# Attention: the narrow transposes of a slot share one PSUM buffer, and the exponentials come first in every slot

## The chip, the cores and the metric

The kernel runs on one core of a Trainium2 chip. The metric is the device time of one execution in microseconds (us). Before the change it is 1161.03 us, the median of three runs (1156.31, 1161.03 and 1164.13).

## The reference, cut to what matters

Attention with a learned bias from relative positions, then two feed-forward blocks on its output (B = 4, H = 8, S = 576, D = 64; 2304 tokens, 512 columns). The change is in the first block alone.

```python
scores = scale * np.matmul(q, k.transpose(0, 1, 3, 2)) + bias
scores = scores - np.max(scores, axis=-1, keepdims=True)
attn = np.exp(scores)
attn = attn / (np.sum(attn, axis=-1, keepdims=True) + 1e-09)
x = np.matmul(attn, v)                       # block 1: attention
h = x @ w_in                                 # block 2
x = (h * np.clip(h + 3.0, 0.0, 6.0) / 6.0) @ w_out
out = (sigmoid(x @ w_gate) * (x @ w_val)) @ w_out2   # block 3
```

## The kernel before, in words

The program has a bias stage (to about 57 us), the attention (57 to about 340 us), the first feed-forward block and the gated one. Attention works on 16 units; a unit n is a pair of heads of one batch. A unit has nine steps s: steps 0 to 7 are a block of 128 query rows of one head (chunk c = s // 2, head h = s % 2), and step 8 holds the last 64 rows of both heads. The 144 steps t run in slots of two: `slot_of_two(i)` (L508) does in slot i, in this order of the text:

- `scores` (L374) of steps 2i and 2i+1: 4 matmuls each (10 for step 8) into a tile `s` of two PSUM banks (two such tiles), then on VectorE (DVE) one custom instruction (L388) that adds the bias into `u` and finds the row's bound. A score tile is free again when its `u` is made.
- In every slot that is in the table `AV` (L498): the 20 matmuls of P times V for half of the query columns of a unit (`av`, L466), and on DVE the product with the inverse sums (`av_out`, L490). Slots with and without this work alternate, but two slots without it follow each other once in nine: modulo 9 the slots 5, 7, 1 and 3 have it. Here they are called AV slots.
- `expo` (L402): the exponential of the slot's two steps on ScalarE (ACT, L404), with the row sums.
- `invert` (L407), one slot after step 5 or 8 of a unit: reciprocal sums on DVE, spread over `spread` by ACT copies (L415).
- `turn_inv` (L417), two slots after step 5 or 8: TensorE (PE) transposes 3 or 2 blocks of `spread` into a PSUM tile `tr`, which ACT and DVE evict to `inv`.
- `trans` (L438) of the two steps of the slot before: 4 transposes of the probabilities `p` (or `pm`, for step 8) into a tile `tr`, evicted to `ptm` by DVE or ACT (the table `PT_EVAC`: steps 1, 3, 5, 7 by ACT, 0, 2, 4, 6 by DVE; step 8 by ACT in odd units).
- `trans_rem` (L454): the narrow rest, one transpose per chunk (and one of `pm` with the fourth chunk), evicted to `ptr`. The rest of chunk 0 of the next unit shares the tile of the second `turn_inv` (`beside`).
- `prep` and `load_qk`: splitting Q and K of the next unit (casts on ACT at L336, products on GpSimd, POOL) and loading those of the one after.

`tr` is a ring of three banks (`bufs=3`): a transpose into a new tile waits until the tile taken three times earlier is evicted. PE's order is that of the text (`in_turn` ties each matmul to the one before). On the other engines a scheduler sets the order at build time. Between these, ten weights of the next block are prepared (`load.one_step`, L689: a DMA `raw`, an `Abs` on ACT at L174, DVE work at L178 to L190, a cast on ACT at L206).

The exponentials have two places: at their place above when the slot is an AV slot or the next is none (L522), and else at the end of the slot, tied behind the last ACT eviction (L543):

```python
        for t in steps(i) if i not in AV and i + 1 in AV else ():
            with ExitStack() as order:
                if last_e:
                    order.enter_context(tc.issue_after(last_e[-1].ins))
                expo(t)
```

Of the kernel before, what the change touches and what calls it, by code (L numbers as in the profile page):

```python
# [10 lines left out]
F32 = mybir.dt.float32  # L11
# [7 lines left out]
P = 128  # L19
B, H, S, D = 4, 8, 576, 64  # L20
# [21 lines left out]

PREP_ON = "APPP"
PT_EVAC = "VAVAVAVAA"


NPRE = 10
# [49 lines left out]
def block_kernel(ctx: ExitStack, tc: tile.TileContext, q, k, v, mlp, w_in, w_out, w_gate, w_val, w_out2, dist_d,  # L97
                 rows_d, out):
    nc = tc.nc
# [253 lines left out]
    ptm = apool.tile([P, 2, 4, S], F32, name="ptm")  # L353
    ptr = apool.tile([P, S], F32, name="ptr")
    pts, us, avs, last_u, last_pe = {}, {}, {}, [None], []
    last_e = []

    @contextmanager
    def in_turn():
# [54 lines left out]
            i = sums[n % 3][:, s0:s1].unsqueeze(2).to_broadcast(o.shape)  # L414
            nc.scalar.copy(o, i)  # L415

    def turn_inv(n, c0, c1):  # L417

        ps = pp.tile([P, 4, P], F32, name="tr", bufs=3)
        for c in range(c0, c1):  # L420
            with in_turn() as done:
                done(nc.tensor.transpose(ps[:, c % 3], spread[:, P * c : P * c + P], ident))
        if c1 == 3:
            evac("A", inv[:, 0 : 3 * P].rearrange("p (c q) -> p c q", c=3), ps[:, 0:3])
        else:
            evac("V", inv[:, 3 * P : 4 * P], ps[:, 0])
            for h in range(2):
                r = slice(64 * h, 64 * h + 64)
                evac("VA"[h], inv[r, 4 * P : S], ps[r, 1, r])
            return ps  # L430

    def evac(eng, dst, src):
        if eng == "A":
            last_e.append(nc.scalar.copy(dst, src))  # L434
        else:
            nc.vector.tensor_copy(dst, src)  # L436

    def trans(t):  # L438
        n, s = seq[t]
        if s < 8:  # L440
            ps = pp.tile([P, 4, P], F32, name="tr", bufs=3)
            c, h = divmod(s, 2)
            for kc in range(4):
                with in_turn() as done:
                    done(nc.tensor.transpose(ps[:, kc], pts[n, c][:, h, 64 * h + P * kc : 64 * h + P * kc + P], ident))  # L445
            evac(PT_EVAC[s], ptm[:, h, :, P * c : P * c + P], ps)
        else:
            ps = pp.tile([P, 4, P], F32, name="tr", bufs=3)
            for kc in range(4):
                with in_turn() as done:  # L450
                    done(nc.tensor.transpose(ps[:, kc], Pm[n % 2][:, P * kc : P * kc + P], ident))
            evac("VA"[n % 2], ptm[:, :, :, 512:S], ps.rearrange("p c (h q) -> p h c q", h=2))

    def trans_rem(n, c, beside=None):  # L454

        ps = pp.tile([P, 4, P], F32, name="tr", bufs=3) if beside is None else beside[:, 2:4]
        with in_turn() as done:
            done(nc.tensor.transpose(ps[:, 0], pts[n, c].rearrange("p h s -> p (h s)")[:, 512 : 512 + P], ident))
        if c == 3:
            with in_turn() as done:  # L460
                done(nc.tensor.transpose(ps[0:64, 1], Pm[n % 2][:, 512:S], ident))
            for h in range(2):
                evac("AV"[h], ptr[64 * h : 64 * h + 64, 512:S], ps[0:64, 1, 64 * h : 64 * h + 64])
        evac("A", ptr[:, P * c : P * c + P], ps[:, 0])

    def av(n, a, g):  # L466
        if g == 0:
# [37 lines left out]
    def steps(i):  # L505
        return [t for t in (2 * i, 2 * i + 1) if 0 <= t < NS]

    def slot_of_two(i):  # L508

        for t in steps(i):  # L510
            scores(t)
            n, s = seq[t]
            p, b = divmod(n, B)
            if s == 0:
                last_v[0] = load_v(n)
            if b == B - 1 and p + 1 < NPAIR and (s % 2 == 1 or s == 8):
                load_bias(p + 1, s // 2)
        for n, a, g in AV.get(i, ()):
            av(n, a, g)
            if g == 4:  # L520
                av_out(n, a)
        for t in steps(i) if i in AV or i + 1 not in AV else ():  # L522
            expo(t)
        for t in steps(i - 1):
            n, s = seq[t]
            if s in (5, 8):
                invert(n, s // 6 * 3, s // 6 * 2 + 3)
        beside = None
        for t in steps(i - 2):
            n, s = seq[t]  # L530
            if s in (5, 8):
                beside = turn_inv(n, s // 6 * 3, s // 6 * 2 + 3)
        for t in steps(i - 1):
            n, s = seq[t]
            trans(t)
            if s in REM and (s < 8 or n % 2 == 0):
                trans_rem(n, REM[s], beside)
                beside = None
        for t in steps(i - 2):
            n, s = seq[t]  # L540
            if s == 8 and n % 2:
                trans_rem(n, REM[s])
        for t in steps(i) if i not in AV and i + 1 in AV else ():  # L543
            with ExitStack() as order:
                if last_e:
                    order.enter_context(tc.issue_after(last_e[-1].ins))
                expo(t)
        for t in steps(i):
            if t in PREP:
                n, h = PREP[t]  # L550
                prep(n, h)
            for k, (n, h) in PREP.items():
                if h == 1 and n + 1 < NU and t == k + 3:
                    load_qk(n + 1)
# [426 lines left out]
```

## Time and profile before

| | us |
|---|---|
| median of three runs | 1161.03 |
| the profiled execution, its own time | 1163.19 |
| its span (first to last instruction) | 1161.4 |
| PE busy in the span | 1121.8 (97%) |
| attention (57 to 340 us): length, PE busy | 283.0, 263.1 |
| attention: ACT busy, DVE busy | 221.5, 211.1 |
| the rest after attention (340 to 1161 us): length, PE busy | 821.0, 813.2 |

The page gives busy time by engine. A view by windows gives the same for a stretch; the list of waits says which engine stood idle until which other engine's instruction ended; the timeline gives the instructions of one engine in order of time, neighbours of a kind merged into one row with a count. "L458" is line 458 of the kernel. A name such as `tr` stands for all buffers of that name. PE's granted clock is 0.99 to 1.00 throughout.

### The profile page before, as it was taken

What the parts mean: (1) busy time and instruction counts of PE and PEld (TensorE: products, weight loads), DVE (VectorE), ACT (ScalarE), POOL (GpSimd) and SP (SyncE); (2) the same over time, 40 slices, a digit from 0 to 9 for tenths busy, and PEclk for the clock granted to TensorE, in tenths of its full rate; (3) what the DMA queues carried; (4) which work ended last, traced back from release to release, by engine and by line L of the source; (5) the groups of instructions that cost most, each with busy time, mean ns of one, the idle gap of its engine ahead of it and who ended that gap; (6) DMA issues with size and microseconds to landing.
All of it is one profiled execution on the core that took longest, in us unless ns stands there. A gap on an engine that the chain in (4) does not pass through costs nothing.

```text
span 1161.4 us, 19270 instructions
## 1 busy us (share of the span) xinstructions
PE 1121.8 (97%) x6878; PEld 1013.5 (87%) x6878; DVE 762.8 (66%) x1487; ACT 585.8 (50%) x1288; POOL 422.8 (36%) x340
## 2 busy tenths in 40 slices
PE   8799999989999999999999999999999999999998
PEld 3287777767779999999999999989899898998997
DVE  8977777787768887356377685575357656643443
ACT  7988877877855455454455445333333222221221
POOL 0154635635206443231346445261333313311211
PEclk9999999999999999999999999999999999999999
DMA  6855436364113565349566659976868748757532
GB/s 203 298 160 143 143 102 194 95 184 128 33 38 109 201 213 194 118 154 327 185 240 233 255 184 347 397 259 256 334 251 303 298 167 312 281 187 258 190 109 73
DMA packets 83503, 236.82 MB, mean 204 GB/s; under 512 B 9936, under 2 KB 12624, under 8 KB 83408
## 3 DMA queue, kind: packets, MB, share of 16 engines
q1 hardware_dynamic: 83408, 235.60, 58.3%
q8 instruction: 54, 0.88, 0.3%
q14 instruction: 41, 0.34, 0.1%
HBM read 154.15 MB, written 81.41 MB: 203 GB/s over the span
## 4 chain that ended last, share of the span: by engine, by line
PE 79%; DVE 6%; ACT 6%; DMA 4%; issue 2%; POOL 1%; SPq 0%; ACTq 0%; POOLq 0%; DVEq 0%
PE o L728 17%; PE h L862 11%; PE o L862 10%; PE o L917 6%; PE h L917 6%; PE h L664 5%; PE h L665 5%; PE h L663 5%; PE s L384 4%; PE av L475 4%; DMA raw<-in_part_dram 3%; PE tr L445 2%; ACT p L404 2%; DVE u L388 2%; DVE ptm L436 1%
## 5 line engine op out<-in xcount | busy, mean ns | idle before, releaser
L728 PE MATMUL o<-gh,slot 128*128 128x384 f32 x768 | 195.9, 335 | 1.8 <-DVE take L436 1.8
L728 PEld LDWEIGHTS o<-gh,slot 128*128 128x128 f32 x768 | 139.2, 188 | 2.2 <-DVE take L436 2.1
L728 PE MATMUL o<-gl,slot 128*128 128x384 f32 x384 | 129.1, 336 | 0.7 <-DVE gl L714 0.7
L388 DVE CUSTOM_DVE_ANT_0 u<-s,bias 128x576 f32<-128x576 f32 x128 | 94.2, 754 | 26.1 <-ACT p L404 12.1
L384 PE MATMUL s<-k,q 128*128 128x288 f32 (+2 forms) x672 | 106.3, 303 | 0.8 <-ACT ptm L610 0.4
L898 POOL TENSOR_TENSOR gp<-s,gp 128x384 fp32r<-128x384 f32 x36 | 39.4, 1107 | 176.8 <-ACT gp L897 91.7
L404 ACT ACTIVATE p<-u,stat 128x576 f32<-128x576 f32 x128 | 98.1, 773 | 11.0 <-DVE stat L388 10.7
L670 DVE SCALAR_TENSOR_TENSOR g<-g,h 128x384 f32<-128x384 f32 x94 | 51.5, 548 | 70.4 <-ACT g L669 70.3
L714 DVE TENSOR_TENSOR gl<-g,gh 128x384 fp32r<-128x384 f32 x94 | 63.2, 672 | 47.9 <-ACT gh L713 46.1
L713 ACT CAST gh<-g 128x384 fp32r<-128x384 f32 x94 | 48.2, 513 | 91.3 <-DVE g L670 91.0
L384 PEld LDWEIGHTS s<-k,q 128*128 128x128 f32 x672 | 91.5, 190 | 1.6 <-DVE stat L388 0.8
L207 POOL TENSOR_TENSOR hl<-corners,hl 128x512 fp32r<-128x512 f32 x42 | 57.3, 1368 | 94.2 <-ACT hl L206 79.2
L669 ACT ACTIVATE g<-h,half 128x384 f32<-128x384 f32 x94 | 54.5, 580 | 58.8 <-PE h L665 58.3
L862 PE MATMUL o<-x,slot 128*128 128x384 f32 x432 | 78.0, 335 | 0.0
L862 PE MATMUL h<-x,slot 128*128 128x384 f32 x432 | 77.8, 335 | 0.0
L862 PEld LDWEIGHTS h<-x,slot 128*128 128x128 f32 x432 | 75.2, 188 | 0.7
L207 POOL TENSOR_TENSOR slot<-z,slot 128x512 fp32r<-128x512 f32 x19 | 28.5, 1503 | 129.7 <-ACT slot L206 129.7
L862 PEld LDWEIGHTS o<-x,slot 128*128 128x128 f32 x432 | 75.1, 188 | 0.0
L445 PE MATMUL tr<-ident,p 128*128 128x128 f32 x512 | 73.3, 277 | 1.4 <-ACT ptr L434 1.3
L728 PEld LDWEIGHTS o<-gl,slot 128*128 128x128 f32 x384 | 72.4, 189 | 1.3 <-DVE gl L714 1.3
L898 POOL TENSOR_TENSOR x<-s,x 128x384 fp32r<-128x384 f32 x36 | 40.2, 1130 | 81.7 <-ACT x L897 48.3
L475 PE MATMUL av<-ptm,vn 128*64 128x288 f32 x512 | 69.2, 413 | 0.0
(154 smaller groups left out, 2708.7 us busy)
## 6 DMA issues: line engine op xcount, KB each, us to landing
w<-hl SPq DMA_DIRECT2D x67, 512.0 KB, 3.4
slot<-w SPq DMA_DIRECT2D x67, 512.0 KB, 5.8
raw<-in_part_dram SPq DMA_DIRECT2D x50, 512.0 KB, 4.2
x<-xc SPq DMA_DIRECT2D x56, 384.0 KB, 5.9
sum<-sum SPq DMA_DIRECT2D x72, 256.0 KB, 3.4
early<-xc SPq DMA_DIRECT2D x28, 384.0 KB, 6.0
nbias<-ptm SPq DMA_DIRECT2D x36, 295.5 KB, 3.1
early<-in_part_dram SPq DMA_DIRECT2D x32, 288.0 KB, 4.4
```

Of the source, the lines that this page charges most:

```text
L207: eng.tensor_tensor(out=slot[:, 1], in0=z, in1=slot[:, 0].bitcast(F32), op=ALU.subtract)
L384: done(nc.tensor.matmul(ps[:, a, o : o + w], Q[:, q0 : q0 + P], K[:, r, h, k0 : k0 + w], start=(i == 0), stop=(i == len(mm) - 1)))
L388: last_u[0] = nc.vector.tensor_tensor_reduce(out=halves(u), in0=ps[:, :, 0:HS], in1=halves(bt), op0=ALU.add, op1=ALU.min, scale=-0.125, sc ...
L404: nc.scalar.activation(probs(t), us.pop(t), AF.Exp, bias=low[n % 2][:, s : s + 1], scale=-1.0, accum_out=sums[n % 3][:, s : s + 1])
L445: done(nc.tensor.transpose(ps[:, kc], pts[n, c][:, h, 64 * h + P * kc : 64 * h + P * kc + P], ident))
L475: done(nc.tensor.matmul(ps[64 * h : 64 * h + 64, 0:HS], vt[:, 4 * h + g], ptm[:, h, g, cols], start=(g == 0), stop=False))
L663: nc.tensor.matmul(ps[:, 0:TW], wh, XH[:, c], start=(c == 0), stop=False)
L714: last_g[0] = nc.vector.tensor_tensor(out=gl, in0=g, in1=gh.bitcast(F32), op=ALU.subtract)
L728: nc.tensor.matmul(os[c][:, 0:TW], sl[:, r, P * c : P * c + P], x, start=(first and r == 0 and x is gh), stop=(last and x is gl))
L862: nc.tensor.matmul(ps[b], sl[:, r, o : o + P], x[:, c, s], start=(k < 4 and i == 0), stop=(i == len(mm) - 1), skip_group_check=True)
L898: nc.gpsimd.tensor_tensor(out=G[:, i, 1], in0=s, in1=G[:, i, 0].bitcast(F32), op=ALU.subtract)
L917: nc.tensor.matmul(os[i], x[:, P * i : P * i + P], slots[(base + 14 + e) % NALL][:, r], start=first, stop=last)
```

## The change

There are three parts. (1) `turn_inv` and `trans_rem` no longer take a tile and evict at once. They are given a tile and a column, do their transposes, and return a function that evicts. `turn_narrow` collects the narrow transposes of a slot in one tile `tr` of four columns, makes all of them, and then does all evictions. (2) Their place moves: the inverse sums now come after the wide transposes of the slot, and for odd units those of step 8 come three slots later rather than two. (3) All exponentials are at their first place, and the tie to the last ACT eviction is gone. No arithmetic is added or left out. Over two units 27 tiles `tr` are taken rather than 28.

```diff
+    def turn_inv(n, c0, c1, ps, at):
         for c in range(c0, c1):
+            turn(ps[:, at + c - c0], spread[:, P * c : P * c + P])
+        def out():
+            if c1 == 3:
+                evac("A", inv[:, 0 : 3 * P].rearrange("p (c q) -> p c q", c=3), ps[:, at : at + 3])
+            else:
+                evac("V", inv[:, 3 * P : 4 * P], ps[:, at])
...
+        return out
...
-    def trans_rem(n, c, beside=None):
-        ps = pp.tile([P, 4, P], F32, name="tr", bufs=3) if beside is None else beside[:, 2:4]
+    def trans_rem(n, c, ps, at):
+        turn(ps[:, at], pts[n, c].rearrange("p h s -> p (h s)")[:, 512 : 512 + P])
         if c == 3:
+            turn(ps[0:64, at + 1], Pm[n % 2][:, 512:S])
+        def out():
+            if c == 3:
+                for h in range(2):
+                    evac("AV"[h], ptr[64 * h : 64 * h + 64, 512:S], ps[0:64, at + 1, 64 * h : 64 * h + 64])
+            evac(REM_EVAC[c], ptr[:, P * c : P * c + P], ps[:, at])
+        return out
...
-        for t in steps(i) if i in AV or i + 1 not in AV else ():
+        for t in steps(i):
             expo(t)
...
-        beside = None
-        for t in steps(i - 2):
-            n, s = seq[t]
-            if s in (5, 8):
-                beside = turn_inv(n, s // 6 * 3, s // 6 * 2 + 3)
+        narrow = []
+        for back in (2, 3):
+            for t in steps(i - back):
+                n, s = seq[t]
+                if s == 5 and back == 2:
+                    narrow.append((3, turn_inv, n, 0, 3))
+                elif s == 8 and back == 2 + n % 2:
+                    narrow.append((2, turn_inv, n, 3, 5))
+                if s == 8 and back == 2 and n % 2:
+                    narrow.append((2, trans_rem, n, 3))
+        def turn_narrow(todo):
+            ps, at, outs = ring_tr(), 0, []
+            for w, f, *what in todo:
+                outs.append(f(*what, ps, at))
+                at += w
+            for out in outs:
+                out()
         for t in steps(i - 1):
             n, s = seq[t]
             trans(t)
             if s in REM and (s < 8 or n % 2 == 0):
-                trans_rem(n, REM[s], beside)
-                beside = None
-        for t in steps(i - 2):
-            n, s = seq[t]
-            if s == 8 and n % 2:
-                trans_rem(n, REM[s])
-        for t in steps(i) if i not in AV and i + 1 in AV else ():
...
+                turn_narrow([(2 if s == 8 else 1, trans_rem, n, REM[s]), *narrow])
+                narrow = []
+        if narrow:
+            turn_narrow(narrow)
```

**PE, slot 15 (two slots after step 8 of unit 2, an even unit).** The names carry the buffers' numbers; `spread` is what the inverse sums are transposed from. Before:

```order
L384 MATMUL s_1427<-k1_231,q1_229 128x288 x4
L422 MATMUL tr_1434<-ident_234,spread_236 128x128 x2
L445 MATMUL tr_1440<-ident_234,p_1355 128x128 x4
L458 MATMUL tr_1434<-ident_234,p_1355 128x128
L445 MATMUL tr_1448<-ident_234,p_1388 128x128 x4
L384 MATMUL s_1463<-k1_231,q1_229 128x288 x4
```

After:

```order
L384 MATMUL s_1426<-k1_231,q1_229 128x288 x4
L422 MATMUL tr_1436<-ident_234,p_1337 128x128 x4
L422 MATMUL tr_1442<-ident_234,p_1337 128x128
L422 MATMUL tr_1442<-ident_234,spread_236 128x128 x2
L422 MATMUL tr_1450<-ident_234,p_1387 128x128 x4
L384 MATMUL s_1462<-k1_231,q1_229 128x288 x4
```

The two transposes of `spread` moved behind the narrow one, into the same tile; the narrow one no longer writes a tile that was being evicted.

**ACT, slots 17 and 18 (step 8 of unit 3, an odd unit, and the slot after).** `q1` is the cast for a later unit, `z` the weight's `Abs`, `pm1` the exponential of step 8. Before:

```order
L404 ACTIVATE p_1493,stat_235<-u_1519,stat_235 128x576
L336 CAST q1_229<-early_222 64x640
L434 COPY ptm_239<-tr_1544 128x4x128
L404 ACTIVATE pm1_233,stat_235<-u_1534,stat_235 128x576
L434 COPY ptr_240<-tr_1550 128x128
L174 ACTIVATE z_1663<-raw_1606 128x512
L434 COPY inv_237<-tr_1582 128x384
L336 CAST q1_229<-early_222 64x576
L434 COPY ptm_239<-tr_1587 128x4x128
L415 COPY spread_236<-stat_235 128x128 x2
L434 COPY ptm_239<-tr_1593 128x8x64
L404 ACTIVATE p_1599,stat_235<-u_1567,stat_235 128x576
```

After:

```order
L404 ACTIVATE p_1492,stat_235<-u_1518,stat_235 128x576
L415 COPY spread_236<-stat_235 128x384
L337 CAST q1_229<-early_222 64x640
L404 ACTIVATE pm1_233,stat_235<-u_1533,stat_235 128x576
L442 COPY ptm_239<-tr_1543 128x4x128
L442 COPY ptr_240<-tr_1549 128x128
L175 ACTIVATE z_1656<-raw_1605 128x512
L404 ACTIVATE p_1577,stat_235<-u_1566,stat_235 128x576
L404 ACTIVATE p_1577,stat_235<-u_1575,stat_235 128x576
L415 COPY spread_236<-stat_235 128x128 x2
L442 COPY ptm_239<-tr_1584 128x4x128
L442 COPY ptm_239<-tr_1590 128x8x64
```

The eviction of step 5 (the first copy to `ptm`) moved behind `spread` and `pm1`, and the two exponentials of slot 18 moved ahead of that slot's evictions.

**ACT, slots 19 and 20 of the same unit, after the change alone.** `tr_1648` is the shared narrow tile of slot 19.

```order
L442 COPY inv_237<-tr_1596 128x384
L404 ACTIVATE p_1633,stat_235<-u_1612,stat_235 128x576
L404 ACTIVATE p_1633,stat_235<-u_1619,stat_235 128x576
L337 CAST q1_229<-early_222 64x576
L442 COPY ptm_239<-tr_1642 128x4x128
L442 COPY ptr_240<-tr_1648 128x128
L442 COPY ptr_240<-tr_1648 64x64
L404 ACTIVATE p_1672,stat_235<-u_1663,stat_235 128x576
L442 COPY ptr_240<-tr_1648 128x128
```

The last eviction of the narrow tile now stands behind an exponential of slot 20, and the second cast of `q1` has come from slot 18 to here.

## Rows read from the trace of the kernel before

**Rows 1.** View by windows: us, busy (x instructions) of PE, PEld, DVE, ACT, POOL, clock, DMA.

```profile
57.00:340.00 283.00, 263.08 (x2046) 213.26 (x2047) 211.06 (x560) 221.53 (x578) 131.18 (x99) 0.99 0.42 122
420.00:745.00 325.00, 325.00 (x1877) 325.00 (x1876) 205.85 (x330) 156.01 (x300) 129.90 (x106) 1.00 0.65 236
```

**Rows 2.** List of waits, 57 to 340 us: us in total, times, longest.

```profile
PE tr L458 <- ACT inv L434: 17.6, 15, 1.7
PE tr L445 <- ACT ptr L434: 1.3, 1, 1.3
DVE ptr L436 <- ACT ptr L434: 8.9, 7, 1.7
```

**Rows 3.** Timeline of PE, unit 2: start, us, instructions, count, [idle before <-releaser].

```profile
109.18 0.60 PE L445 MATMUL tr<-ident,p 128*128 128x128 f32 x4
111.06 0.33 PE L458 MATMUL tr<-ident,p 128*128 128x128 f32 x1 [1.28 <-ACT inv L434]
```

**Rows 4.** Timelines of DVE and ACT, same place.

```profile
109.69 0.75 DVE L388 CUSTOM_DVE_ANT_0 u<-s,bias 128x576 f32<-128x576 f32 x1
110.36 0.41 DVE L436 COPY inv<-tr 128x128 f32<-128x128 f32 x2
110.81 0.21 ACT L434 COPY inv<-tr 64x64 f32<-64x64 f32 x1 [0.40 <-DVE inv L436]
```

**Rows 5.** Timeline of PE, odd units: the first, unit 3 and the last of seven waits.

```profile
92.84 0.44 PE L458 MATMUL tr<-ident,p 128*128 128x128 f32 x2 [0.63 <-ACT inv L434]
...
119.07 1.30 PE L384 MATMUL s<-k,q 128*128 128x288 f32 x8
120.22 0.49 PE L422 MATMUL tr<-ident,spread 128*128 128x128 f32 x3
...
121.38 1.29 PE L384 MATMUL s<-k,q 128*128 128x288 f32 x8
...
125.18 0.44 PE L422 MATMUL tr<-ident,spread 128*128 128x128 f32 x2
...
127.81 0.44 PE L458 MATMUL tr<-ident,p 128*128 128x128 f32 x2 [1.10 <-ACT inv L434]
...
305.92 0.44 PE L458 MATMUL tr<-ident,p 128*128 128x128 f32 x2 [0.96 <-ACT inv L434]
```

**Rows 6.** Timeline of ACT, unit 3, slots 17 to 19.

```profile
118.03 0.78 ACT L404 ACTIVATE p<-u,stat 128x576 f32<-128x576 f32 x1 [1.07 <-DVE stat L388]
...
118.80 0.71 ACT L336 CAST q<-early 64x640 fp32r<-64x640 f32 x1
119.42 0.58 ACT L434 COPY ptm<-tr 128x512 f32<-128x512 f32 x1
119.90 0.77 ACT L404 ACTIVATE pm<-u,stat 128x576 f32<-128x576 f32 x1
...
121.52 0.67 ACT L174 ACTIVATE z<-raw 128x512 f32<-128x512 f32 x1 [0.60 <-DMA raw<-in_part_dram]
122.10 0.45 ACT L434 COPY inv<-tr 128x384 f32<-128x384 f32 x1
122.45 0.67 ACT L336 CAST q<-early 64x576 fp32r<-64x576 f32 x1
123.03 0.57 ACT L434 COPY ptm<-tr 128x512 f32<-128x512 f32 x1
123.51 0.49 ACT L415 COPY spread<-stat 128x128 f32<-128x128 f32 x2
123.90 0.57 ACT L434 COPY ptm<-tr 128x512 f32<-128x512 f32 x1
124.38 0.77 ACT L404 ACTIVATE p<-u,stat 128x576 f32<-128x576 f32 x1
```

**Rows 7.** ACT's groups, 57 to 340 us: count, busy us, mean ns, idle before.

```profile
L434 ACT COPY ptr<-tr 128x128 f32<-128x128 f32 x64 | 17.0, 266 | 10.2 <-DVE ptr L436 6.7 <-PE tr L458 3.5
L415 ACT COPY spread<-stat 128x384 f32<-128x384 f32 x16 | 8.0, 500 | 0.0
```

More of the change, by code (lines that the diff above doesn't have):

```diff
@@ L44 @@
 PT_EVAC = "VAVAVAVAA"
+REM_EVAC = "AAAA"
 NPRE = 10
@@ L355, in block_kernel @@
     pts, us, avs, last_u, last_pe = {}, {}, {}, [None], []
-    last_e = []
     @contextmanager
@@ L415, in invert, with ring_tr, turn @@
             nc.scalar.copy(o, i)
-    def turn_inv(n, c0, c1):
-        ps = pp.tile([P, 4, P], F32, name="tr", bufs=3)
-        for c in range(c0, c1):
[L421 to L430, printed above, removed]
+    def ring_tr():
+        return pp.tile([P, 4, P], F32, name="tr", bufs=3)
+    def turn(out, x):
+        with in_turn() as done:
+            done(nc.tensor.transpose(out, x, ident))
+    def turn_inv(n, c0, c1, ps, at):
+        for c in range(c0, c1):
+            turn(ps[:, at + c - c0], spread[:, P * c : P * c + P])
[5 more added lines that the diff above has]
+                for h in range(2):
+                    r = slice(64 * h, 64 * h + 64)
+                    evac("VA"[h], inv[r, 4 * P : S], ps[r, at + 1, r])
+        return out
     def evac(eng, dst, src):
         if eng == "A":
-            last_e.append(nc.scalar.copy(dst, src))
+            nc.scalar.copy(dst, src)
         else:
@@ L439, in trans @@
         n, s = seq[t]
+        ps = ring_tr()
         if s < 8:
-            ps = pp.tile([P, 4, P], F32, name="tr", bufs=3)
             c, h = divmod(s, 2)
             for kc in range(4):
-                with in_turn() as done:
-                    done(nc.tensor.transpose(ps[:, kc], pts[n, c][:, h, 64 * h + P * kc : 64 * h + P * kc + P], ident))
+                turn(ps[:, kc], pts[n, c][:, h, 64 * h + P * kc : 64 * h + P * kc + P])
             evac(PT_EVAC[s], ptm[:, h, :, P * c : P * c + P], ps)
         else:
-            ps = pp.tile([P, 4, P], F32, name="tr", bufs=3)
             for kc in range(4):
-                with in_turn() as done:
-                    done(nc.tensor.transpose(ps[:, kc], Pm[n % 2][:, P * kc : P * kc + P], ident))
+                turn(ps[:, kc], Pm[n % 2][:, P * kc : P * kc + P])
             evac("VA"[n % 2], ptm[:, :, :, 512:S], ps.rearrange("p c (h q) -> p h c q", h=2))
-    def trans_rem(n, c, beside=None):
-        ps = pp.tile([P, 4, P], F32, name="tr", bufs=3) if beside is None else beside[:, 2:4]
-        with in_turn() as done:
-            done(nc.tensor.transpose(ps[:, 0], pts[n, c].rearrange("p h s -> p (h s)")[:, 512 : 512 + P], ident))
+    def trans_rem(n, c, ps, at):
+        turn(ps[:, at], pts[n, c].rearrange("p h s -> p (h s)")[:, 512 : 512 + P])
         if c == 3:
[L460 to L464, printed above, removed]
+            turn(ps[0:64, at + 1], Pm[n % 2][:, 512:S])
+        def out():
+            if c == 3:
+                for h in range(2):
+                    evac("AV"[h], ptr[64 * h : 64 * h + 64, 512:S], ps[0:64, at + 1, 64 * h : 64 * h + 64])
+            evac(REM_EVAC[c], ptr[:, P * c : P * c + P], ps[:, at])
+        return out
     def av(n, a, g):
@@ L527, in slot_of_two @@
                 invert(n, s // 6 * 3, s // 6 * 2 + 3)
-        beside = None
-        for t in steps(i - 2):
-            n, s = seq[t]
-            if s in (5, 8):
-                beside = turn_inv(n, s // 6 * 3, s // 6 * 2 + 3)
+        narrow = []
[13 more added lines that the diff above has]
+                at += w
+            assert at <= 4
+            for out in outs:
+                out()
         for t in steps(i - 1):
@@ L536, in slot_of_two @@
             if s in REM and (s < 8 or n % 2 == 0):
-                trans_rem(n, REM[s], beside)
-                beside = None
-        for t in steps(i - 2):
-            n, s = seq[t]
-            if s == 8 and n % 2:
-                trans_rem(n, REM[s])
-        for t in steps(i) if i not in AV and i + 1 in AV else ():
[L544 to L547, printed above, removed]
+                turn_narrow([(2 if s == 8 else 1, trans_rem, n, REM[s]), *narrow])
+                narrow = []
+        if narrow:
+            turn_narrow(narrow)
         for t in steps(i):
```

## The prediction

> **What bounds the kernel now.** I read the windows first, then the list of waits, then the timelines around the longest wait. The windows [rows 1] show that the attention is 283.0 us long and PE is busy in 263.1 of them, while ACT has 221.5 and DVE 211.1. So PE sets the stage, with 19.9 us of idle time. After it PE has next to no idle time: in the window from 420 to 745 us it is busy throughout. What the attention gains, the kernel gains, since the later stages begin behind PE's last attention matmul and keep their length; the weights that they need first are prepared during the attention by ACT, DVE and POOL, which all have room there.
>
> The list of waits [rows 2] says what the idle time is: 17.6 of the 19.9 us, in 15 waits, are one thing. The narrow transpose at L458 waits for ACT's eviction to `inv`. Both use one tile: `turn_inv` has filled it, and its evictions must be done before `trans_rem` may write the remaining columns. This happens once per unit, except in the last one.
>
> The timelines show two kinds of wait. In even units [rows 3] PE is done with the wide transposes at 109.78 (109.18 and 0.60) and starts the narrow one at 111.06, after 1.28 us. What it waits for is a queue on DVE [rows 4]: the second `u` of the slot starts at 109.69, the two evictions to `inv` only at 110.36, and ACT's part of the same bank follows at 110.81. In odd units [rows 5] it is a queue on ACT: seven waits from 0.63 to 1.11 us, the first at 92.84, the last at 305.92, 1.10 in unit 3; the seven sum to 6.5 us, so the eight of even units are 17.6 - 6.5 = 11.1 us. In unit 3 [rows 6] ACT works without a gap from the weight's `Abs`, which waits 0.60 us for its DMA and starts at 121.52, through evictions, a cast and four exponentials up to the eviction that PE waits for, and PE goes on at 127.81.
>
> **The change part by part.**
>
> *The shared tile, transposes before evictions.* No transpose writes a tile that is being evicted any more, so all 15 waits go as they stand: -17.6 us. The matmuls are the same ones, one tile fewer is taken per two units, and the number of evictions is unchanged. What remains is the ring: the narrow tile must be free, three tiles back, and the probabilities must be there.
>
> *Even units: what is late next.* Without the wait PE comes to the scores of the next slot 1.28 us sooner. They need the two score tiles, which are free when the slot's two `u` are made: at 109.69, and at 110.36 to 110.44 [rows 4]. PE would start the first four matmuls at about 110.3 and the second four at half of a score block (1.15 us from 119.07 to 120.22 [rows 5]) later, about 110.9. So there are some 0.4 us in hand on the second tile, and the next transposes lie behind an AV slot's scores and products, which take 3.80 us (121.38 to 125.18 [rows 5]). I take no new wait here: -11.1 us for the eight even units. The evictions of the inverse sums now stand later on DVE; the product that reads `inv` comes at the end of the next slot, so this is hidden by those 3.80 us of PE work. The same holds for the inverse sums of odd units, which are made one slot later and still one slot before the product.
>
> *Odd units: the order on ACT.* Here I follow ACT and PE with the new order and the durations of unit 3 [rows 6, 7]; a step costs its start to the next one's start, so an exponential 0.77, a cast 0.62 or 0.58, a copy of 512 columns 0.48 (0.58 to its end). The first exponential of slot 17 starts at 118.03. Before, its cast and the eviction of step 5 followed, which ended at 119.42 + 0.58 = 120.00, just ahead of PE's next use of that bank at 120.22. Now `spread` (0.50, less the 0.10 by which neighbouring copies overlap, so 0.40) and `pm` (0.77) stand ahead too: 118.03 + 0.77 + 0.40 + 0.62 + 0.77 = 120.59, and the end of the copy is 121.17. PE wants the bank for the first wide transposes of slot 18 at 120.22, because the inverse sums no longer take it. That is a new wait of 0.95 us. It is on record in the order for units 3, 5, 7 and 9; in units 1, 11 and 13 the eviction stands ahead of `pm`, and I take nothing.
>
> From there PE is 0.95 us late, and ACT goes on: `Abs` at 121.52 (its DMA does not depend on this), then two exponentials, `spread`, two wide evictions, `inv`, two exponentials, the second cast, a wide eviction and two short ones of the narrow tile: 121.52 + 0.58 + 1.54 + 0.39 + 0.96 + 0.35 + 1.54 + 0.58 + 0.48 + 0.31 = 128.25. The last eviction of the narrow tile stands behind an exponential of slot 20. Its scores start at 121.38 + 0.95 + 3.80 + 11 transposes of 0.105 (11 take 1.16 from 120.22 to 121.38) = 127.29; half of them 0.58, `u` 0.75, the exponential 0.77, and the copy 0.27 give 129.66. PE wants that bank for the narrow transposes of slot 20 at 127.29 + 1.15 + 0.84 = 129.28: a second new wait of about 0.4 us. Units 11 and 13 have this one too (about 0.4 and, with two more casts ahead, 0.5); in unit 1 the last eviction stands ahead of the exponential and I take nothing. So odd units get 4 x 1.35 + 0.9 = 6.3 us back, against 6.5 us that went. The change of place on ACT costs there what the shared tile gains.
>
> Nothing in rows shows how far ACT's new order holds in the other units, so I bound these waits: zero, if ACT is less late there than in unit 3 (its queue starts later than usual because of the DMA), and 7 x (0.95 + 0.4) = 9.5 us if all odd units behave like unit 3. I keep 6.3, from the orders as they stand.
>
> A rule speaks against sharing a tile. The rows show evictions of one bank by two engines one behind the other: DVE waited 8.9 us in 7 cases for ACT's eviction to `ptr` [rows 2], and ACT 6.7 us for DVE's [rows 7]. The Trainium skill, PSUM — Partial Sum Buffer, section "PSUM bank collisions raise a hardware error", says that no two engines may access the same bank and quadrant at once, even to read different columns, so accesses are to be ordered by bank. By that rule, which the trace agrees with, a tile with more contents is released later, by the sum of its evictions; if the two engines could drain it side by side, the last copy would end near 128.5, ahead of PE, and the time would come out some 1.9 us lower.
>
> *The exponentials first.* 30 slots are concerned (each before an AV slot). The number of exponentials is the same. They issue no DMA. Behind them on ACT stand the evictions of the slot, later by two exponentials, 1.54 us; the slot that follows is an AV slot, where PE has 3.80 us of scores and products before it needs the banks. That hides it, at no cost, except where two slots without products follow each other, which is the odd case above. The cast that moved from slot 18 to 20 delays POOL's products for a unit that starts two slots later still, and the load on SP behind them; POOL is busy 131.2 of 283 us [rows 1], so I cost this at nothing. If that cover failed, it would show as scores waiting for POOL.
>
> The sum: -11.1 (even) - 6.5 + 6.3 (odd) = -11.3 us. Against the profiled execution's own time, 1163.19 (span 1161.4 and 1.8 around it), that is 1151.9; it was 2.2 us above the median, so for the median I take 1161.03 - 11.3 = 1149.7 us.
>
> **The rivals.** (a) All waits go and none returns: ACT is busy in only 221.5 of the then 264 us, and its exponentials are spread more evenly, which also lets the wait of 1.3 us go that stands alone in [rows 2]. Time: 1161.0 - 17.6 - 1.3 = 1142.1. Against it stands the order of units 3 to 9. (b) Even units give only half: DVE's queue, which set the wait of 1.28 us, is as long as before, and the margin of 0.4 us on the score tile is eaten by work that runs slower beside POOL. Half of the mean of 1.39 us, eight times, is 5.6 us back: 1155.3. For it speaks that the wait ended on DVE; against it that the two `u` stand ahead of `inv` in DVE's order. (c) Slower: evictions behind exponentials starve the ring. In each of the 30 slots the evictions come 1.54 us later, and the banks have only the margin seen at 120.22 (0.22 us after 120.00). That is 30 x 1.32 = 39.6 us, less 17.6: +22.0, so 1183.0. It decides as soon as a moved slot costs PE more than 17.6 / 30 = 0.59 us. Against it: each of these slots is followed by the 3.80 us of an AV slot.
>
> **How the numbers follow.** A measurement of this kernel tells about 1% from no change. My forecast has a chance of 0.45, with a range of its own from 1145 to 1154 (odd units costing between nothing and 9.5 us); all waits gone 0.17; half in the even units 0.29, some of it down to no gain at all; slower 0.09, of which a part stays within 1%. The bound of 1% below is 1149.4, so the forecast's mass is split about evenly by it: faster 0.17 + 0.23 + 0.05 = 0.45, slower 0.07, within 1% 0.48. The range reaches from the case in which all goes to just under no change: 1141 to 1160.
>
> **What would show it.** In the profile after, the waits of a narrow transpose for ACT `inv` should be gone, the even places should run from wide transposes through the narrow ones to scores without a gap, and the attention should end near 329 us rather than 340, with the later stages as long as before. New waits of a transpose for ACT `ptm` of about 0.95 us should stand in the slot after step 8 of units 3, 5, 7 and 9, and waits for ACT `ptr` of about 0.4 us two slots later. The prediction is wrong in its mechanism if even places show waits for the score tiles, if the odd units show no new waits, or if the gain is lost after the attention.

## The result, and the profile after

The kernel after took 1148.76 us (median of 4 runs, 1148.01 to 1149.37), the kernel before, run beside it, 1162.52 us (4 runs, 1156.31 to 1164.13). The ratio is 0.989, with a 95% interval from 0.985 to 0.993. The forecast was 1149.7 us, in a range from 1141 to 1160. It stood on a gain of 11.3 us from 1161.03 us; measured are 12.3 us from there and 13.8 us from the runs beside it.

The profiled execution of the kernel after has a span of 1147.0 us, against 1161.4. Its windows over the attention and over the later stage answer to [rows 1]; the columns are the same.

```profile
57.00:329.00 272.00, 263.85 (x2061) 213.40 (x2062) 216.33 (x564) 222.78 (x578) 132.81 (x100) 1.00 0.43 127
420.00:745.00 325.00, 325.00 (x1877) 325.00 (x1876) 201.89 (x325) 155.07 (x299) 128.88 (x107) 1.00 0.67 242
```

PE does the same attention work (263.9 us, before 263.1) in a stretch that is 11 us shorter. The last products with `ptr` start at 329.94, before at 343.20: 13.3 us earlier. What follows is as long as before (about 817 us from there to the end of either span), and PE is still busy throughout from 420 to 745 us. So the whole change of the span, 14.4 us, lies in the attention but for 1.1 us. Those are one wait late in the last block: PE waited 1.5 us for ACT's `x` before, and 0.4 us after (list of waits).

The list of waits of PE from 57 to 330 us, beside [rows 2]:

```profile
PE tr L422 <- ACT ptr L442: 4.0, 7, 0.9
PE tr L422 <- ACT ptm L442: 3.0, 6, 0.5
PE s L384 <- DVE stat L388: 0.7, 2, 0.4
PE tr L422 <- DVE ptm L444: 0.3, 1, 0.3
```

The 17.6 us for ACT's eviction to `inv` are gone as a kind. With a few short ones up to 345 us, all PE waits sum to 8.9 us (before 20.2); 0.9 of the 8.9 us belong to the next block already. The even place of unit 2, PE's timeline beside [rows 3]:

```profile
106.22 0.71 PE L422 MATMUL tr<-ident,p 128*128 128x128 f32 x5
106.76 0.38 PE L422 MATMUL tr<-ident,spread 128*128 128x128 f32 x2
106.98 0.60 PE L422 MATMUL tr<-ident,p 128*128 128x128 f32 x4
107.50 1.48 PE L384 MATMUL s<-k,q 128*128 128x288 f32 x8
```

The wide four, the narrow one and the two of the inverse sums follow each other without a gap, then the next four, then scores. Where 1.28 us stood there is no wait. The scores bring a little of their own in this unit: they start at 107.50, right behind the end of the `u` that frees their tile (107.44 on DVE), and the eight take 1.48 us, against 1.30 in [rows 5]. It costs 0.33 us here (the interval of unit 2 below is 7.47 us, that of six other even units 7.14), and the list, which counts a wait from the end of the matmul ahead, doesn't show it.

Unit 3, an odd one, PE's timeline beside [rows 5]:

```profile
115.16 1.46 PE L384 MATMUL s<-k,q 128*128 128x288 f32 x8
116.46 0.62 PE L422 MATMUL tr<-ident,p 128*128 128x128 f32 x4
117.58 0.66 PE L422 MATMUL tr<-ident,pm 128*128 128x128 f32 x4 [0.51 <-ACT ptm L442]
...
127.37 0.33 PE L422 MATMUL tr<-ident,p 128*128 128x128 f32 x1 [0.53 <-ACT ptr L442]
```

and ACT's beside [rows 6]:

```profile
115.15 0.52 ACT L415 COPY spread<-stat 128x384 f32<-128x384 f32 x1 [0.16 <-DVE stat L411]
115.57 0.72 ACT L337 CAST q<-early 64x640 fp32r<-64x640 f32 x1
116.19 0.77 ACT L404 ACTIVATE pm<-u,stat 128x576 f32<-128x576 f32 x1
...
116.96 0.56 ACT L442 COPY ptm<-tr 128x512 f32<-128x512 f32 x1
...
119.64 0.69 ACT L175 ACTIVATE z<-raw 128x512 f32<-128x512 f32 x1 [1.95 <-DMA raw<-in_part_dram]
120.23 0.76 ACT L404 ACTIVATE p<-u,stat 128x576 f32<-128x576 f32 x1
```

The eviction to `ptm` stands behind `spread`, the cast and `pm`, as the order said; it ends at 117.52, and PE's second four wide transposes, those of `pm`, go on at 117.58. The first four, at 116.46, did not wait. The wait of 0.53 at 127.37 is the second one that was foretold. Two more, of 0.55 us at 122.75 and 0.47 us at 126.18, both for ACT's `ptm`, stand in unit 3 alone: there `Abs` waited 1.95 us for its DMA, 0.60 before, and the evictions stand behind it.

To see where the time went, I took from PE's timeline the interval between the starts of successive groups of products with `ptr` (32 groups, 31 intervals). They repeat in fours: one that holds an even unit's narrow place, one with step 8 of an odd unit, the next one, which holds that unit's last narrow transposes, and one of 7.73 us that no kernel changes. The table gives the sums over the eight units, the start of the last group, PE's waits from 57 to 345 us by the list, and the median of the runs.

| kernel | even | odd, step 8 | odd, next | last group | waits | median |
|---|---|---|---|---|---|---|
| before | 74.1 | 76.9 | 66.2 | 343.2 | 20.2 | 1161.1 |
| after | 59.1 | 82.1 | 63.4 | 329.9 | 8.9 | 1148.8 |
| tiles only | 61.8 | 83.3 | 64.9 | 335.9 | 10.7 | 1155.6 |
| exponentials first only | 79.8 | 76.9 | 63.7 | 345.7 | 20.4 | 1165.7 |
| tile of its own | 65.1 | 78.0 | 69.5 | 338.4 | 14.4 | 1155.8 |
| tile of its own, exponentials first | 74.2 | 78.0 | 63.6 | 341.3 | 18.9 | 1159.2 |
| after, odd units not late | 57.7 | 82.2 | 65.4 | 330.9 | 10.0 | 1149.8 |
| after, evictions ahead | 59.7 | 81.9 | 62.7 | 329.8 | 7.2 | 1149.2 |
| after, rest on ACT | 57.7 | 80.7 | 60.6 | 324.6 | 5.4 | 1145.5 |

From before to after: even -15.0, step 8 of odd units +5.2, the next -2.8, and the first group starts 0.6 earlier: -13.2. The kernel before had medians from 1160.5 to 1162.5 us on the chips used; each ratio below is to its runs on the same chip.

### The profile page after: what moved, and what is told of

It is laid out like the page before. It is cut to its first block, busy times and chain, and to the rows that moved or that the text cites. A ratio compares the mean times of both kernels' runs of the same rounds, so it can differ in the third digit from the quotient of the medians.

```text
span 1147.0 us, 19230 instructions
## 1 busy us (share of the span) xinstructions
PE 1120.0 (98%) x6878; PEld 1012.1 (88%) x6878; DVE 768.1 (67%) x1487; ACT 586.6 (51%) x1288; POOL 424.6 (37%) x340
## 4 chain that ended last, share of the span: by engine, by line
PE 81%; ACT 5%; DVE 4%; DMA 3%; issue 2%; POOL 2%; SPq 0%; ACTq 0%; POOLq 0%; DVEq 0%
PE o L743 17%; PE h L877 11%; PE o L877 11%; PE o L932 6%; PE h L932 6%; PE h L679 5%; PE h L678 5%; PE h L680 5%; PE tr L422 4%; PE s L384 4%; PE av L482 4%; ACT p L404 2%; DMA raw<-in_part_dram 1%; PE av L487 1%; DVE u L388 1%
## 5 line engine op out<-in xcount | busy, mean ns | idle before, releaser
L422 PE MATMUL tr<-ident,p 128*128 128x128 f32 x576 | 81.0, 277 | 5.0 <-ACT ptr L442 4.0
L422 PEld LDWEIGHTS tr<-ident,p 128*128 128x128 f32 x576 | 64.6, 141 | 18.1 <-ACT ptr L442 5.6
```

What stands on the lines that cost most here:

```text
L422: done(nc.tensor.transpose(out, x, ident))
```

## The experiments

**The two halves of the change, each alone.** The first keeps the change's tiles and puts the exponentials back where they were:

```diff
-        for t in steps(i):
+        for t in steps(i) if i in AV or i + 1 not in AV else ():
             expo(t)
...
+        for t in steps(i) if i not in AV and i + 1 in AV else ():
+            with ExitStack() as order:
+                if last_e:
+                    order.enter_context(tc.issue_after(last_e[-1].ins))
+                expo(t)
```

> The shared narrow tiles and their place as in the change, but the exponentials late as before, tied behind the slot's last ACT eviction in the slots ahead of an AV slot. Theory (the gain is the 15 waits for ACT's inv, which the shared tile takes away; the place of the exponentials adds nothing): no wait of a transpose for inv in even units, new waits in odd units of the same size or somewhat larger than after the change, time 1146 to 1152 us. Rival (half or more of the gain comes from the exponentials, which spread ACT's work more evenly): 1154 us or more, with waits in even units.

Measured: 1155.63 us (5 runs), ratio 0.995 (0.993 to 0.997): less than half of the gain. The time is the rival's, but of the even units, which it expected to wait, only unit 10 has waits in the list. No wait for `inv` is left; others stand there. The list of waits, and from unit 3 PE's and ACT's timelines:

```profile
PE tr L423 <- ACT p L405: 4.0, 2, 2.2
```

```profile
125.28 1.63 PE L423 MATMUL tr<-ident,p 128*128 128x128 f32 x10 [2.24 <-ACT p L405]
```

```profile
122.04 0.68 ACT L175 ACTIVATE z<-raw 128x512 f32<-128x512 f32 x1 [3.52 <-DMA raw<-in_part_dram]
...
124.33 0.80 ACT L405 ACTIVATE p<-u,stat 128x576 f32<-128x576 f32 x1
```

Here `Abs` waited 3.52 us for its DMA, and the slot's first exponential started only 2.3 us behind it, after four evictions and copies; PE waited 2.24 us for the probabilities, and 1.78 us at the like place of unit 7. In the kernel after, the exponential follows `Abs` at once (119.64, 120.23), and these waits are not there. The two intervals are 3.2 us longer than in the kernel after (10.53 and 10.09 us, against 9.36 and 8.04), of the 5.9 us by which the attention ends later. Why the DMA lands later here was not tried. Another 1.3 us are in unit 11, where PE waits 1.38 us for a score tile (0.40 after). The rest is spread, among others over the even intervals (7.75 to 7.98 in four units, 7.14 to 7.47 after); no wait in the list names its cause, and it stays open.

The second has the kernel before with the exponentials first:

```diff
-        for t in steps(i) if i in AV or i + 1 not in AV else ():
+        for t in steps(i):
             expo(t)
...
-        for t in steps(i) if i not in AV and i + 1 in AV else ():
-            with ExitStack() as order:
-                if last_e:
-                    order.enter_context(tc.issue_after(last_e[-1].ins))
-                expo(t)
```

> The exponentials first in every slot, the tiles and evictions as before the change. Theory: the waits for ACT's inv stay, about 1.3 us in each even unit (DVE's queue sets them) and about 0.6 to 1.3 in odd ones, 14 to 18 us in all, time 1158 to 1165 us. Rival (the exponentials bring the gain): the waits fall to half or less, 1153 us or less.

Measured: 1165.68 us (10 runs), ratio 1.004 (1.003 to 1.006). The waits:

```profile
PE tr L458 <- ACT inv L434: 20.1, 14, 2.4
```

The rival is refuted, and the time lies just above the theory's range. In even units the wait grew from 1.3 to 1.93 us, since the eviction to `inv` now stands behind two exponentials. But in odd units it fell (4.1 us in all, 6.5 before), and in sum PE's waits are as long as before (20.4 and 20.2 us in the table), so they don't hold the 4.6 us. What differs is the clock. In this profile PE's granted clock fell to 0.50 three times in the attention (from 148, 254 and 325 us on), before once (last section). And the two of the ten runs with a mean clock of 0.996 took 1163.1 and 1163.3 us, as the three runs of before at 0.996 did (1163.0 to 1163.5); the other eight had 0.992 to 0.994, lower than any of the 22 of before on that chip. So the halves do not add: -5.4 and +4.6 alone, -13 to -14 together.

**The shared tile without a change of order.** The kernel before, with the rest of a unit's narrow columns in a tile of its own, so that nothing is written into a tile under eviction:

```diff
-                trans_rem(n, REM[s], beside)
-                beside = None
+                trans_rem(n, REM[s])
```

> The kernel before, but the rest of chunk 0 gets a tile of its own rather than the free columns of the inverse sums' tile, so no tile is written while it is evicted; 29 tiles per two units rather than 28. Theory (what counts is when a bank comes free in a ring of three, so a fourth tile in the slot meets the same eviction): the wait for inv moves to another transpose of the same slot and stays at 0.9 to 1.5 us in even units, 12 to 19 us in all, time 1157 to 1167 us. Rival (the wait is only the one shared tile, and a tile more would have done): the waits fall below 6 us, time 1150 us or less.

Measured: 1155.83 us (8 runs), ratio 0.996 (0.994 to 0.997). The time lies between the ranges of theory and rival. The expectation that the wait stays fell for even units. (The edit takes 30 tiles per two units, not 29: the rest of chunk 0 gets one in odd units too.) The waits:

```profile
PE tr L458 <- ACT inv L434: 5.5, 7, 1.1
PE tr L445 <- ACT ptm L434: 4.5, 8, 0.6
```

Odd units still wait for `inv` (0.48 to 1.09 us), even units 0.57 us instead of 1.3, at the second wide transposes: the slot now takes four tiles from a ring of three, and the fourth needs a bank of the same slot. Here it is not that of the inverse sums, whose evictions come later (from 109.82 on), but that of the first wide transposes, which ACT evicts at once. PE and ACT in unit 2:

```profile
109.60 0.66 PE L445 MATMUL tr<-ident,p 128*128 128x128 f32 x4 [0.57 <-ACT ptm L434]
```

```profile
108.96 0.59 ACT L434 COPY ptm<-tr 128x512 f32<-128x512 f32 x1 [0.83 <-PE tr L445]
```

Some 5 us of this row of the table are unit 3 alone: its interval is 13.32 us, with waits of 0.42, 0.92 and 1.09 us and a clock of 0.50 from 128 to 133 us; in units 1 and 5 it is 8.1 us.

**Both: a tile of its own and the exponentials first.** The two edits above in one kernel.

> This is the kernel before with two edits: the rest of chunk 0 goes into a tile of its own instead of the tile of the inverse sums, and the exponentials stand first in every slot. The two were run apart: the tile of its own alone took 5 us off (1155.8 against 1161.1), the exponentials alone added 4.6 us (1165.7). Theory A: the loss by the exponentials alone came from the wait for inv, whose eviction they push back; with a tile of its own that wait is gone in even units, so the exponentials now cost nothing or gain there, as they do in the changed kernel: 1149 to 1154, hardly any wait of a transpose for inv in even units and the remaining waits on ACT's odd slots. Theory B: the two edits simply add, so the exponentials cost 4.6 us here too, 1159 to 1162, and the gain of the changed kernel hangs on its ring having one tile fewer.

Measured: 1159.16 us (10 runs), ratio 0.999 (0.998 to 1.000). The time is theory B's. The list of waits, and PE's and ACT's timelines in unit 2:

```profile
PE tr L445 <- ACT inv L434: 12.8, 7, 1.8
```

```profile
111.87 0.66 PE L445 MATMUL tr<-ident,p 128*128 128x128 f32 x4 [1.83 <-ACT inv L434]
```

```profile
109.95 0.77 ACT L404 ACTIVATE p<-u,stat 128x576 f32<-128x576 f32 x1 [1.13 <-DVE stat L388]
...
110.73 0.76 ACT L404 ACTIVATE p<-u,stat 128x576 f32<-128x576 f32 x1
...
111.61 0.21 ACT L434 COPY inv<-tr 64x64 f32<-64x64 f32 x1
```

The fourth tile of the slot needs the bank of the first here, and its eviction stands behind both exponentials. With three tiles in the slot, as the kernel after has them, an eviction may stand there: its bank is asked for only in the next slot. So the exponentials cost nothing after and some 3 to 4 us here. That the number of tiles alone decides this is argued: the kernel after also puts the inverse sums behind the wide transposes, and no run takes the two apart.

**The slot's delay in odd units.** The kernel after, with the inverse sums of odd units in their old slot, in a tile of their own:

```diff
-                elif s == 8 and back == 2 + n % 2:
+                elif s == 8 and back == 2 and n % 2 == 0:
                     narrow.append((2, turn_inv, n, 3, 5))
...
+        for t in steps(i - 2):
+            n, s = seq[t]
+            if s == 8 and n % 2:
+                turn_narrow([(2, turn_inv, n, 3, 5)])
         for t in steps(i - 1):
```

> This is the changed kernel with one part undone: the inverse sums of odd units are transposed in their old slot again, ahead of the wide transposes and in a ring tile of their own. Theory A: the waits of 0.50 us of the second wide transposes in the slot after step 8 of units 3, 5, 7 and 9, and those of 0.53 to 0.57 us two slots later, exist because one tile fewer stands in the ring there; with the tile back these waits go but the odd slots then wait for the additional tile instead (as the kernel before did for 0.63 to 1.10 us at its narrow transpose), so the attention gains nothing: 1147 to 1152. Theory B: the delay by a slot is what makes the odd units good; without it each odd unit loses the 0.9 us that it lost before: 7 x 0.9 = 6.3, 1153 to 1157.

Measured: 1149.80 us (4 runs), ratio 0.991 (0.989 to 0.993). The time is theory A's, its mechanism only half: the waits of 0.50 stayed (`ptm`: 2.0 us in 4), and where `ptr` had 4.0 us, waits of a transpose for `inv` stand now:

```profile
PE tr L422 <- ACT inv L442: 5.8, 7, 1.6
```

In the table the interval after step 8 loses 2.0 us, the even ones gain 1.4: the delay is worth about 1 us, which the runs (1149.8 and 1148.8 us, on two chips) don't tell from nothing.

**ACT's order in odd units.** The kernel after, with two ties: the exponential `pm` of odd units goes behind the eviction of step 5, and the exponentials of the slot after an odd unit's shared narrow tile behind its last eviction:

```diff
         for t in steps(i):
-            expo(t)
+            if t not in behind:
+                with ExitStack() as order:
+                    if rest_e:
+                        order.enter_context(tc.issue_after(rest_e[-1].ins))
+                    expo(t)
...
+            if s == 5 and behind:
+                with tc.issue_after(last_e[-1].ins):
+                    expo(behind.pop())
```

> The changed kernel with two ties on ACT: in odd units the exponential of step 8 stands behind the eviction of step 5, and the exponentials of the slot after the shared narrow tile of an odd unit stand behind that tile's last eviction. Theory (the new waits of odd units are the order on ACT, 3.0 us for ptm and about 3 of the 4.0 for ptr): both groups go or fall to a third, time 1142 to 1146 us. Rival (ACT is short of time there in any order, so the wait reappears at the next transpose that needs p): waits of 5 us or more stay in sum, time 1147 to 1150 us.

Measured: 1149.16 us (6 runs), ratio 0.990 (0.988 to 0.992), so no different from after: the rival's time. The attention ends 0.2 us sooner, and the intervals of step 8 in units 3 to 9 stay at 10.7 us. What a transpose no longer waits is waited elsewhere: in unit 5 the second wide transposes start 0.77 us behind the first instead of 1.12, but the eight scores ahead of them take 1.66 us instead of 1.35 (start to the next start), and the even intervals of units 4, 6 and 8 grew from 7.14 to 7.47 us.

**The bank that two engines evict.** The kernel after, with both 64-column copies of a unit's last narrow columns on ACT:

```diff
-                    evac("AV"[h], ptr[64 * h : 64 * h + 64, 512:S], ps[0:64, at + 1, 64 * h : 64 * h + 64])
+                    evac("AA"[h], ptr[64 * h : 64 * h + 64, 512:S], ps[0:64, at + 1, 64 * h : 64 * h + 64])
```

> This is the changed kernel with both short evictions of the last narrow columns to ptr on ACT, where one stood on DVE and the two engines waited for each other at one bank. Theory A: the waits of a narrow transpose for ACT's ptr (4.0 us in 7) come from this chain, ACT standing behind DVE: they go nearly all, 1144.5 to 1147.5, and the single wait of 0.94 us in unit 10 goes with them. Theory B: ACT's own queue sets these waits (exponential and cast ahead of the copy); the additional copy on ACT, about 0.15 us, makes them as long or longer: 1148 to 1151.

Measured: 1145.53 us (4 runs), ratio 0.987 (0.983 to 0.990): theory A. What it takes away is seen in the kernel after at unit 10. Timelines of DVE, ACT and PE there:

```profile
241.58 1.64 DVE L179 TENSOR_SCALAR z<-z 128x512 f32<-128x512 f32 x1
243.26 0.22 DVE L444 COPY ptr<-tr 64x64 f32<-64x64 f32 x1
```

```profile
243.51 0.27 ACT L442 COPY ptr<-tr 128x128 f32<-128x128 f32 x1 [1.86 <-DVE ptr L444]
```

```profile
243.83 0.33 PE L422 MATMUL tr<-ident,p 128*128 128x128 f32 x1 [0.94 <-ACT ptr L442]
```

PE waited for ACT, ACT for DVE, and DVE was at work on a weight. Of the 15 like instructions in the attention the median takes 0.42 us; POOL worked on `q` from 240.00 to 242.94 meanwhile. In the kernel after run again it is the same (1.66 us at 242.41, POOL until 243.78). That POOL held DVE up is likely, but was not tried. The groups of ACT's long copies to `ptr`, after and then with the rest on ACT (count, busy, mean ns, idle before):

```profile
L442 ACT COPY ptr<-tr 128x128 f32<-128x128 f32 x64 | 16.9, 264 | 5.9 <-DVE ptr L444 5.9
```

```profile
L442 ACT COPY ptr<-tr 128x128 f32<-128x128 f32 x64 | 17.0, 266 | 0.2
```

The 5.9 us that ACT waited for DVE's copy became 0.2, and of PE's waits in the attention the list keeps only

```profile
PE tr L422 <- ACT ptm L442: 2.2, 5, 0.5
PE s L384 <- DVE stat L388: 2.0, 2, 1.7
```

**The same once more, beside the kernel after and a combination with the two ties.**

> The kernel with both short evictions on ACT once more, beside the changed kernel on the same chip, to see whether it beats it beyond doubt. If the chain between the two engines was what it removed, it stays 2.5 to 5 us under the changed kernel; if that difference came from the chip, the two agree within 1 us.

> The changed kernel as it is, on the same chip as the two others: 1147.5 to 1150, 10 to 14 us under the kernel before.

> This is the changed kernel with both short evictions of the last narrow columns on ACT, and the two ties on ACT's order (exponentials behind the wide eviction in odd units, and behind the last eviction of the shared narrow tile). Without the ties, the short evictions on ACT gave 1145.5 and left 2.2 us of waits for ACT's ptm and 2.0 us of scores for DVE; the ties alone gave nothing. Theory A: ACT's load sets the odd units, so the ties move the wait again and change nothing: 1144 to 1147. Theory B: with the chain between the two engines gone, the ties can take the 2.2 us of waits for ptm as well: 1142 to 1144.

Measured on one chip: rest on ACT 1144.81 us (1144.06 to 1145.64), the kernel after 1148.20 (1146.99 to 1149.14), rest on ACT with the ties 1146.14 (1143.82 to 1146.73), four runs each. So the rest on ACT is 3.4 us better than the kernel after, without an overlap of the runs, and the ties add nothing. Its attention gains more: the last group starts 5.4 us sooner by the table and 5.8 us in this pair. Late in the last block, PE's wait for ACT's `x` takes 1.8 us of it back (2.2 us, 0.4 in the kernel after, in both pairs of profiles). So what the attention gains is not all handed on.

## Why the prediction was right

**The bound.** PE set the attention, the 17.6 us were one cause, and the gain passed through to the end unchanged: held. The table shows the last group 13.3 us earlier and the span 14.4 us shorter. It is no rule: of the 5.4 us that the rest on ACT gains beyond this, 1.8 are lost behind the attention.

**Even units, -11.1.** The waits went, and the scores behind the even places brought back 0.33 us, in unit 2 alone, so the rival by which half comes back (5.6 us) is refuted. The even intervals gained 15.0. A typical one went from 8.65 to 7.14, which is 1.5 rather than 1.39. The term was sized by the list, which counts a wait from the end of the matmul ahead. A transpose lasts 0.27 us in the trace, while the next of a row starts 0.11 us after it does, so some 0.16 us of such a wait aren't listed. The largest interval, 11.58 in unit 4, held longer waits and a stretch of halved clock (below), which the sum didn't contain either. Unit 10 gained little more than the typical ones: it was 1.94 us above them before, and is 1.68 above them after, with a wait of 0.94 us for `ptr`.

**Odd units, -6.5 + 6.3.** The first new wait came where it was put, in units 3, 5, 7 and 9, but as 0.50 us instead of 0.95. The failed step is the tile: PE wants that bank not for the first wide transposes of the slot but for the second, those of `pm`, four transposes later (0.44 us at the step of 0.11). I had taken the ring to go round strictly, each tile in the bank of the one taken three times earlier, as the section on the kernel has it. It does not: the first four were written at 116.46, while the tile three before was evicted only from 116.96 on. The wait two slots later was 0.53 to 0.57 in five units, forecast as 0.4, and 0.23 in unit 13, forecast as 0.5.

Yet the sum was too kind: by the table odd units lost 2.4 us, forecast as a gain of 0.2. The interval of step 8 grew by 0.9 in units 3 to 9, of which only 0.5 is a wait in the list. PE's starts show the rest. Before, the two rows of wide transposes follow each other after 0.44 us:

```profile
120.54 0.60 PE L445 MATMUL tr<-ident,p 128*128 128x128 f32 x4
120.98 0.65 PE L451 MATMUL tr<-ident,pm 128*128 128x128 f32 x4
```

After, it is 1.12 us in unit 3 (116.46 to 117.58), so the wait costs 0.68. The eight scores ahead of them take 1.30 us to the next start (115.16 to 116.46), before 1.15 (119.07 to 120.22): the second four are late for their tile. In units 1 and 13, which grew by 0.2, the same transposes are 0.17 us late, which the list doesn't show. In unit 11 the interval grew by 1.2 us, with waits of 0.40 us for a score tile and 0.34 us for a copy on DVE; the sum had neither.

**The order of evictions of one bank.** The rule of the Trainium skill (PSUM — Partial Sum Buffer, section "PSUM bank collisions raise a hardware error") was read as making the shared tile leave later, by the sum of its evictions. The trace agreed: ACT waited 5.9 us for DVE at `ptr`. The run with both copies on ACT adds what such a chain costs: 3.4 us of the time, and by the table 4.2 us in the intervals of odd units and 1.4 in those of even ones (1.2 of it in unit 10). I had put it at 1.9 us, in odd units alone. That number was not worked out: the second waits, which would go, are 4 x 0.4 + 0.9 = 2.5 us in the sum.

**The exponentials first, at no cost.** Right for the pair, wrong as a statement on the edit: alone it cost 4.6 us (with no more waiting in sum, but at a lower clock), and beside a tile of its own some 3 to 4. The cover I named, the products of the next slot, failed where the slot asked for more tiles than the ring has. No scores waited for POOL. That the edit also takes the exponentials from behind the evictions that follow a waiting `Abs` I had not seen; the tiles alone lack it, and gave only 5.4 us.

**The rivals.** All waits gone (1142.1) did not come about: 8.0 us remain in the attention, 5.0 of them at the places named. It is nearly reached by the version with the rest on ACT (1144.8). Starved ring (1183.0): refuted; the list has 13 waits for ACT's evictions, of 0.54 us in the mean, and not 30 of 1.32. That the time came out 0.9 us from the forecast is luck in part, since two errors stand against each other: the gain of even units was put 3.9 us too low, that of odd units 2.6 too high.

## What to carry to other kernels

A wait for a tile under eviction is won only in part by a tile more (5 of 13 us here), if the ring is as short as the slot is full: count the tiles of a slot against the ring, and look which bank each one gets, before the order on the evicting engine is changed. An order that was free in one layout of the tiles cost time in another. Two edits that lean on each other have to be run apart and together. And a bank that two engines drain is as late as the busier one; 0.2 us of copying moved to the engine that drains the rest was worth 3.4 us here.

## What the runs showed of the hardware

PE's waits can cost more than their length. The clock of 0.99 to 1.00 named ahead is a mean over long stretches. In the kernel before, PE stood for 0.56 and 1.68 us in unit 4 (timeline of PE), and the windows of 1 us behind it, columns as in [rows 1], show the granted clock at 0.50, its level of 1.2 GHz:

```profile
144.63 0.41 PE L422 MATMUL tr<-ident,spread 128*128 128x128 f32 x2 [0.56 <-DVE ptm L436]
...
147.42 0.47 PE L458 MATMUL tr<-ident,p 128*128 128x128 f32 x1 [1.68 <-ACT inv L434]
...
148.40 2.27 PE L384 MATMUL s<-k,q 128*128 128x288 f32 x8
```

```profile
146.00:147.00 1.00, 0.00 (x0) 0.00 (x0) 1.00 (x6) 0.36 (x1) 0.00 (x0) 1.00 0.80 252
147.00:148.00 1.00, 0.58 (x3) 0.58 (x4) 0.89 (x4) 0.27 (x2) 0.00 (x0) 0.70 1.03 247
148.00:149.00 1.00, 1.00 (x6) 1.00 (x5) 0.21 (x1) 1.00 (x4) 0.00 (x0) 0.50 0.41 88
```

The eight scores from 148.40 took 2.27 us, where eight took 1.30 in [rows 5]. What that costs shows best in the kernel with a tile of its own and exponentials first: of seven waits of 1.82 or 1.83 us at the same place of a unit, the clock fell behind one, in unit 6, and its interval was 10.82 us against 9.20, so 1.6 us. With the exponentials first alone, it fell behind three of the eight waits of 1.93 to 2.43 us; with a tile of its own alone, beside waits of 0.42, 0.92 and 1.09 us. Which of like waits it strikes I can't say from these runs. The runs of the kernel before bear it out: on one chip the four of 22 with a mean clock of 1.000 took 1156.6 to 1159.2 us, the three with 0.996 took 1163.0 to 1163.5. Over all chips, eight runs of before at 1.000 have a mean of 1158.3 us, three of after 1147.7. So I estimate that 10 to 11 of the 13 to 14 us are the waits themselves, and the rest lower clock that no longer follows them; no run isolates this.
